# Attention with a threshold and a gated feed-forward: softmax tiles turned before they are normalised, the inverted sums sent through DRAM

## The chip, the cores and the metric

The kernel runs on one core of one Trainium2 chip. The metric is the time of one execution on the device in microseconds (us), the median of several runs. The engines are PE (TensorE; PEld is its weight load), DVE (VectorE), ACT (ScalarE), POOL (GpSimd) and SP (SyncE, which issues nearly all DMAs here).

## The reference

Eight batches, eight heads, 576 tokens, 64 elements a head; then a feed-forward from 512 to 1024 and back to 512 with a gate made by a convolution over three tokens.

```python
scores = scale * np.matmul(q, k.transpose(0, 1, 3, 2))
thresh = np.max(scores, axis=-1, keepdims=True) - tau
scores = np.where(scores >= thresh, scores, -1000000000.0)
scores = scores - np.max(scores, axis=-1, keepdims=True)
attn = np.exp(scores)
attn = attn / (np.sum(attn, axis=-1, keepdims=True) + 1e-09)
return np.matmul(attn, v).astype(np.float32)
...
h = np.maximum(x @ w_in, 0.0)
conv_out += conv_w[k][None, None, :] * hp[:, k:k + S, :]     # three taps over the tokens
gate = 1.0 / (1.0 + np.exp(-conv_out))
return (h * gate @ w_out).astype(np.float32)
```

A row in which no score reaches the threshold gets the same weight for every token.

## The kernel before, in words

**Tiles.** The 576 tokens of a batch are four tiles of 128 rows and one of 64. A batch is two chunks: the tiles 0 and 1 (256 rows), and the tiles 2, 3 and 4 (320 rows). The heads go in pairs, four pairs a batch; with a chunk a pair makes one of 64 entries `i` of the list `pairs`, and each of its tiles is a unit `u` (160 units). In a unit:

- `ps_s`: PE makes the scores of each of two heads (128 x 576, in PSUM; two buffers). In the first batch ("plain") q and k are used as float32, with the batches after that q and k are split in a high and a low part (`xq`, `q1`, `q2`, `ks`), whose pieces SP loads and moves.
- `few`: DVE takes each row's maximum (`top`, L599) and the threshold (`limit`, L605, on DVE, POOL or ACT). ACT makes the exponentials `em` (`exp`, L608), DVE multiplies with the comparison to the threshold and adds up the row (`mask`, L611).
- `guard` (L628), the reciprocal (L635) and `even` (L632) make a factor and, for empty rows, an addend; `norm` (L644, on POOL for 285 of 288 heads) applies both to `em`, in place.
- `transposes` (L703): PE turns `em` in blocks of 128 into `ps_t` (two buffers in PSUM), ACT copies them to `eT` (L698). In 28 units (`crossed`) it goes another way: ACT and POOL split `em` into its low and high 16 bits (`parts`, L326 and L328), SP stores them in DRAM (`rows`) and turns them by a DMA transpose into `eT`.

When all tiles of a pair are turned, `attend` multiplies `eT` with `v` into `pa` (L758, L767). `pa` takes its PSUM buffers from the same two as `ps_t`, and after the first two chunks two pairs go together (pairs 26 and 27, say), so both are in use then. ACT rounds the product into the high part of `x` (L774), DVE subtracts to get the low part (L777), and the buffer is free. With the four pairs of a chunk in `x`, `mm1` (`ph`, L795), the taps and gates (`hp`, `t`, L810 to L822), `gh`/`gl` and `mm2` (`po`, L853) make the feed-forward of that chunk, while the attention of the next runs.

**What sets the order.** `Plan` records every operation with its engine, its cost in ns, what it reads and writes, and a rank; `run` then simulates the engines with these costs and writes the instructions of each engine in the order that comes out. On the chip each engine and SP's queue go through their own list in that order. A buffer taken from a pool in turn (`em`, `few`, `ps_t`, ...) must be free first; operations with `other` may go to another engine when their own has more than a set amount waiting.

Of the kernel before, what the change touches and what calls it, by code (L numbers as in the profile page):

```python
# [10 lines left out]
F32 = mybir.dt.float32  # L11
# [9 lines left out]
HUGE = 3.0e38  # L21
AHEAD = {'s': 6.25, 's4': 7.75, 't': 3.5, 'a': 3.5, 'prep': 4.25, 'w': 2.5, 'load': 7.75}
# [5 lines left out]
NORM = (('pool',), ('pool',))  # L28

NEAR = 8  # L30
# [21 lines left out]
FAR = 3  # L52
XKS = 3
EMS = 5
# [200 lines left out]
def tile_tau_attention_gated_ffn(  # L255
# [307 lines left out]
    def unit(u, k, q1, q2, o, n):  # L563
# [7 lines left out]
        few = plan.buf(sm, "few", 4, [P, 8], F32, f"few_{u}")  # L571
        a = AHEAD["s" if 2 * n > P else "s4"]
        tiny = [("pool", 200)]
        for h, js in enumerate(heads):
            ps = plan.buf(ps_s, "ps_s", 2, [P, 2, 512], F32, f"ps_s_{u}_{h}")
            nm, th, total = (slice(at + h, at + h + 1) for at in (0, 2, 4))
# [33 lines left out]
            def mask(ps=ps, th=th, view=view, total=total):  # L610
                nc.vector.scalar_tensor_tensor(  # L611
                    view(), ps[:rows, :, :CH], few[:rows, th], view(), op0=ALU.is_ge, op1=ALU.mult,
                    accum_out=few[:rows, total]
# [9 lines left out]
            op("dve", 738, mask, w=[(em, h), (few, ("sum", h))], r=[(ps, 0), (few, ("th", h))], ahead=a)  # L623
        ss = [(few, ("sum", h)) for h in range(m)]
        sums, inverse, shift = slice(4, 4 + m), slice(6, 6 + m), slice(2, 2 + m)

        def guard(e):
            engines[e].tensor_scalar(few[:rows, inverse], few[:rows, sums], 1e-9, 1.0, op0=ALU.add, op1=ALU.mult)  # L628


        def even(e):
            engines[e].tensor_scalar(few[:rows, shift], few[:rows, sums], 0.0, 1.0 / S, op0=ALU.is_equal, op1=ALU.mult)  # L632

        op("dve", 112, guard, w=[(few, "inverse")], r=ss, ahead=a, port=True, other=tiny)
        op("dve", 82, lambda: nc.vector.reciprocal(few[:rows, inverse], few[:rows, inverse]), w=[(few, "inverse")], ahead=a)  # L635
        op("dve", 124, even, w=[(few, "shift")], r=ss, ahead=a, port=True, other=tiny)
        for h in range(m):
            def norm(e, h=h):
                sl = em[:rows, h * S:(h + 1) * S]
                by, to = few[:rows, 6 + h:7 + h], few[:rows, 2 + h:3 + h]  # L640
                if e == "act":
                    nc.scalar.activation(sl, sl, AF.Identity, scale=by, bias=to)
                else:
                    engines[e].tensor_scalar(sl, sl, by, to, op0=ALU.mult, op1=ALU.add)  # L644

            choice = {"pool": 807, "dve": 400, "act": 625}
            turns = NORM[u >= NEAR]
            home = turns[(u * 2 + h) % len(turns)]
            op(
# [368 lines left out]
```

## Time and profile before

| | |
|---|---|
| Median of three runs | 923.61 us (923.4 to 923.7) |
| Profiled execution | 925.83 us; its span, from the first to the last instruction, 924.0 us |
| PE, PEld | 883.6 us (96%), 709.9 us (77%) |
| DVE, ACT, POOL | 775.4 us (84%), 684.6 us (74%), 636.5 us (69%) |
| Granted TensorE clock | mean 0.989 |
| DMA | 122.28 MB in 120,927 packets, mean 132 GB/s |

The profile is one execution. A group's row gives line, engine, operation, output <- inputs with their shapes, the count, then busy us and mean ns of one, then the idle time of the engine before them with what ended it. A timeline row gives start, length and instruction, and in brackets the idle time before it with its releaser. A row of waits gives the sum, the number and the longest. DMA rows end with the median us from issue to landing.

### The profile page before, as it was taken

Reading aid. Unit: us, or ns where it says so; the run is one execution under the profiler, and the core shown is the slowest. Engines: PE = TensorE matmul, PEld = TensorE weight load, DVE = VectorE, ACT = ScalarE, POOL = GpSimd, SP = SyncE. Lnnn points to the kernel's source line nnn. Section 1 sums busy time; section 2 is a strip of 40 time slices with the busy share of each in tenths; the row PEclk is TensorE's granted clock in tenths of the full one; section 3 lists DMA queues with packets and bytes.
Section 4 is the critical chain, followed back from the end, with each engine's and each line's share of the span. In section 5 each row is a group of like instructions: output and inputs, shape, how many; then the busy total and the mean of one; then the engine's idle time right before and its main releaser. Section 6 shows DMA issues by size and latency. Waiting matters only on the chain.

```text
span 924.0 us, 18493 instructions
## 1 busy us (share of the span) xinstructions
PE 883.6 (96%) x6056; PEld 709.9 (77%) x6056; DVE 775.4 (84%) x1863; ACT 684.6 (74%) x1450; POOL 636.5 (69%) x1044
## 2 busy tenths in 40 slices
PE   5879899999999999999899999999999999999998
PEld 2445578768879788878778788887868878887897
DVE  5989999988998789987789779996979879998543
ACT  5868688778877787878668687877857778786643
POOL 3656867877777677876667778886866858785422
PEclk9989999999999999999899999999999999999999
DMA  5545137546563565526645275536647076543000
GB/s 207 168 152 158 44 113 210 120 132 181 141 172 76 153 178 158 148 73 175 166 123 126 86 183 138 158 92 181 169 114 180 29 194 169 131 120 100 14 23 35
DMA packets 120927, 122.28 MB, mean 132 GB/s; under 512 B 72320, under 2 KB 88960, under 8 KB 120832
## 3 DMA queue, kind: packets, MB, share of 16 engines
q1 hardware_dynamic: 119968, 119.20, 47.7%
q10 hardware_dynamic: 864, 1.90, 0.6%
q8 instruction: 49, 0.80, 0.4%
q14 instruction: 46, 0.38, 0.1%
HBM read 66.22 MB, written 25.95 MB: 100 GB/s over the span
## 4 chain that ended last, share of the span: by engine, by line
PE 63%; DVE 12%; ACT 10%; POOL 6%; DMA 5%; issue 4%; SPq 1%; ACTq 0%; DVEq 0%; POOLq 0%
PE po L853 17%; PE ph L795 13%; PE pa L767 10%; PE ps_s L591 9%; PE ps_t L703 9%; DVE em L611 4%; ACT em L608 3%; PE ps_s L584 3%; DVE few L599 3%; DMA xq<-in_qd_dram 2%; ACT eT L698 2%; POOL em L644 2%; PE pa L758 2%; DVE t L817 2%; DVE t L822 2%
## 5 line engine op out<-in xcount | busy, mean ns | idle before, releaser
L644 POOL TENSOR_SCALAR em<-em,few 128x576 f32<-128x576 f32 x285 | 258.5, 915 | 34.0 <-DVE few L635 22.4
L611 DVE SCALAR_TENSOR_TENSOR em<-ps_s,few,em 128x576 f32<-128x576 f32 x288 | 230.6, 812 | 38.2 <-ACT em L608 25.4
L608 ACT ACTIVATE em<-ps_s,few 128x576 f32<-128x576 f32 x288 | 210.4, 741 | 51.7 <-DVE few L599 43.1
L599 DVE TENSOR_REDUCE few<-ps_s 128x1 f32<-128x576 f32 x288 | 212.3, 749 | 35.5 <-PE ps_s L591 17.3
L795 PE MATMUL ph<-x,w1h 128*128 128x322 f32 (+1 forms) x1024 | 240.0, 306 | 0.9 <-ACT hp L810 0.6
L698 ACT ACTIVATE eT<-ps_t 128x512 f32<-128x512 f32 (+2 forms) x360 | 168.2, 487 | 31.2 <-PE ps_t L703 28.3
L795 PEld LDWEIGHTS ph<-x,w1h 128*128 128x128 f32 x1024 | 175.6, 191 | 6.3 <-issue 3.2
L703 PE MATMUL ps_t<-ident,em 128*128 128x128 f32 x1060 | 160.3, 280 | 9.6 <-POOL em L644 5.0
L591 PE MATMUL ps_s<-ks,q 128*128 128x288 f32 x896 | 158.9, 307 | 8.5 <-DVE em L611 5.9
L703 PEld LDWEIGHTS ps_t<-ident,em 128*128 128x128 f32 x1060 | 126.2, 143 | 34.4 <-POOL em L644 14.6
L795 PE MATMUL ph<-x,w1l 128*128 128x322 f32 (+1 forms) x512 | 151.9, 297 | 0.0
L591 PEld LDWEIGHTS ps_s<-ks,q 128*128 128x128 f32 x896 | 129.9, 190 | 26.7 <-issue 7.4
L333 POOL TENSOR_TENSOR gl<-t,gh 128x255 fp32r<-128x255 f32 (+9 forms) x192 | 122.7, 652 | 27.9 <-ACT gh L832 26.5
L767 PE MATMUL pa<-eT,v 128*64 128x320 f32 (+1 forms) x1024 | 132.1, 409 | 0.0
L853 PE MATMUL po<-w2h,gh 128*128 128x512 f32 x288 | 119.0, 413 | 0.4 <-ACT hp L810 0.4
L767 PEld LDWEIGHTS pa<-eT,v 128*64 128x64 f32 x1024 | 70.3, 137 | 59.4 <-issue 15.9
L853 PE MATMUL po<-w2h,gl 128*128 128x512 f32 x288 | 113.6, 395 | 0.2
L853 PE MATMUL po<-w2l,gh 128*128 128x512 f32 x288 | 113.5, 394 | 0.0
L817 DVE SCALAR_TENSOR_TENSOR t<-hp,cr 128x321 f32<-128x321 f32 (+1 forms) x128 | 85.1, 668 | 20.2 <-ACT hp L810 20.1
L795 PEld LDWEIGHTS ph<-x,w1l 128*128 128x128 f32 x512 | 97.7, 191 | 0.3
L817 DVE SCALAR_TENSOR_TENSOR t<-hp,cr,t 128x321 f32<-128x321 f32 (+1 forms) x128 | 91.9, 719 | 0.4
L824 ACT ACTIVATE t<-t,cm 128x321 f32<-128x321 f32 (+1 forms) x128 | 68.3, 534 | 28.3 <-DVE t L817 17.6
(81 smaller groups left out, 1147.9 us busy)
## 6 DMA issues: line engine op xcount, KB each, us to landing
v<-in_vc_dram SPq DMA_DIRECT2D x64, 288.0 KB, 3.9
rows<-parts SPq DMA_DIRECT2D x28, 576.0 KB, 3.2
k<-in_kp_dram SPq DMA_DIRECT2D x35, 320.0 KB, 3.5
out_dram<-ot SPq DMA_DIRECT2D x36, 256.0 KB, 2.1
xq<-in_qd_dram SPq DMA_DIRECT2D x28, 320.0 KB, 3.7
xk<-in_kt_dram SPq DMA_DIRECT2D x28, 288.0 KB, 3.3
ks<-xk SPq DMA_DIRECT2D x56, 144.0 KB, 3.6
xq<-in_qd_dram SPq DMA_DIRECT2D x28, 256.0 KB, 3.7
```

The costliest lines, as they stand in the source:

```text
L333: engines[e].tensor_tensor(dst, x, y, op=ALU.subtract)
L591: nc.tensor.matmul(ps[:, c, :CH], lhsT=q[:, h, o:o + n], rhs=k[:, h, c * CH:(c + 1) * CH], start=(i == 0), stop=(i == 1))
L599: nc.vector.tensor_reduce(few[:rows, nm], ps[:rows, :, :CH], op=ALU.max, axis=mybir.AxisListType.XY, negate=True)
L608: nc.scalar.activation(view(), ps[:rows, :, :CH], AF.Exp, bias=few[:rows, nm])
L611: nc.vector.scalar_tensor_tensor(view(), ps[:rows, :, :CH], few[:rows, th], view(), op0=ALU.is_ge, op1=ALU.mult, accum_out=few[:rows, total])
L644: engines[e].tensor_scalar(sl, sl, by, to, op0=ALU.mult, op1=ALU.add)
L698: "act", act(w, True), lambda dst=dst, src=src: nc.scalar.activation(dst(), src(pt), AF.Copy),
L703: nc.tensor.transpose(out=pt[:, at:at + P], in_=em[:, int(b * P):int(b * P) + P], identity=ident[:])
L767: nc.tensor.matmul(pa[j * D:(j + 1) * D, :w], lhsT=vt[:, blk, :], rhs=eT[:, :w // D, blk, :], start=False, stop=(r == 3))
L795: nc.tensor.matmul(ph[:, :an], lhsT=w1[w][:, cb, fs], rhs=xs[cb][:, h, :an], start=(cb == 0 and i == 0), stop=(cb == NCB - 1 and i == 2))
L817: nc.vector.scalar_tensor_tensor(t[:, :kn], hp[:, k:kn + k], cr[:, j, f:f + 1], y, op0=ALU.mult, op1=ALU.add)
L853: nc.tensor.matmul(po[:], lhsT=x[:, f, at:at + P], rhs=w[:, f, :], start=(f == 0 and i == 0), stop=(f == NFB - 1 and i == 2))
```

## The change

The row sums of a pair's units go into one small tile `tot` (a column for each head and tile) instead of each unit's `few`. `norm`, `even` and the per-unit guard and reciprocal go; PE turns `em` as it stands after `mask`. When a pair's units are recorded, `invert` adds a small number to all sums of the pair and inverts them (once a pair, 64 times); two DMAs (four with the chunk of 320 rows) store the columns as rows in DRAM, element by element, and two more load them back, each spread over the 64 partitions of one head (`inv`). In `attend`, DVE multiplies `pa` by `inv` into `xn` in SBUF, ACT rounds that into the high part of `x`, and POOL (or DVE) subtracts to get the low part. For empty rows ACT adds 2^-80 as it copies from `ps_t`; in the crossed units POOL takes the maximum of the high 16 bits with those of 2^-80, in place of a copy. There are four buffers of `em` instead of five.

```diff
+EVEN = 2.0 ** -80
+EVEN_TOP = 0x1780
-NORM = (('pool',), ('pool',))
-NEAR = 8
+INVS = 2
+PARTS = 2
-EMS = 5
+EMS = 4
@@ unit
                 nc.vector.scalar_tensor_tensor(
                     view(), ps[:rows, :, :CH], few[:rows, th], view(), op0=ALU.is_ge, op1=ALU.mult,
-                    accum_out=few[:rows, total]
+                    accum_out=tot[:rows, total]
                 )
...
-        op("dve", 112, guard, w=[(few, "inverse")], r=ss, ahead=a, port=True, other=tiny)
-        op("dve", 82, lambda: nc.vector.reciprocal(few[:rows, inverse], few[:rows, inverse]), w=[(few, "inverse")], ahead=a)
-        op("dve", 124, even, w=[(few, "shift")], r=ss, ahead=a, port=True, other=tiny)
-        for h in range(m):
-            def norm(e, h=h):
...
+    def invert(i, p, n, tot):
+        cols, a = 2 * (n // P) + (n % P > 0), AHEAD["a"]
+        spread = plan.buf(wk, "inv", INVS, [P, S - QW], F32, f"inv_{i}")
+        row = plan.buf(far, "row", INVS, [2, S - QW], F32, f"row_{i}")
+        ts = [(tot, j) for j in range(cols)]
         def guard(e):
+            engines[e].tensor_scalar(tot[:, :cols], tot[:, :cols], S * EVEN, 1.0, op0=ALU.add, op1=ALU.mult)
+
+        op("dve", 112, guard, w=ts, ahead=a, port=True, other=[("pool", 200)])
+        op("dve", 82, lambda: nc.vector.reciprocal(tot[:, :cols], tot[:, :cols]), w=ts, ahead=a)
+        for h in range(2):
+            def out(h=h):
+                nc.sync.dma_start(
+                    row[h, :n // P * P].rearrange("(t q) -> q t", q=P), tot[:, :n // P * 2].rearrange("q (t h) -> q t h", h=2)[:, :, h]
+                )
+
+            op("sp", 500, out, w=[(row, h)], r=ts, ahead=a, ring=n // P * P * 1.6)
+            if n % P:
+                op(
+                    "sp", 500, lambda h=h: nc.sync.dma_start(row[h, n // P * P:n].rearrange("(q e) -> q e", e=1), tot[h * D:(h + 1) * D, cols - 1:cols]),
+                    w=[(row, 2 + h)], r=ts, ahead=a, ring=D * 1.6
+                )
+        for h in range(2):
+            j = h ^ p % 2
+            put(
+                n, lambda h=h, j=j: nc.sync.dma_start(spread[j * D:(j + 1) * D, :n], row[h:h + 1, :n].broadcast_to([D, n])),
+                issue=500, rows=D, w=[(spread, j)], r=[(row, h)] + ([(row, 2 + h)] if n % P else []), ahead=a
             )
-        return em
+        return spread
@@ cross
-                copy(e, parts[:, j], src)
+                if j:
+                    engines[e].tensor_scalar(parts[:, j], src, EVEN_TOP, None, op0=ALU.max)
+                else:
+                    copy(e, parts[:, j], src)
@@ transposes
-                    "act", act(w, True), lambda dst=dst, src=src: nc.scalar.activation(dst(), src(pt), AF.Copy),
+                    "act", act(w, True), lambda dst=dst, src=src: nc.scalar.activation(dst(), src(pt), AF.Copy, bias=EVEN),
@@ attend
-            op("act", act(w, True), high, w=[(x, 0)], r=[(pa, 0)], ahead=a)
-            op("dve", dve(w), low, w=[(x, 1)], r=[(pa, 0), (x, 0)], ahead=a)
+            op("dve", dve(w), scale, w=[(xn, 0)], r=[(pa, 0), (inv, 0), (inv, 1)], ahead=a)
+            op("act", act(w), high, w=[(x, 0)], r=[(xn, 0)], ahead=a)
+            op("pool", pool(w), low, w=[(x, 1)], r=[(xn, 0), (x, 0)], ahead=a, other=[("dve", dve(w))], port=True)
@@ at the last tile of a pair
-                waiting.append((i, p, eT, vts[i], x, off))
+                waiting.append((i, p, eT, vts[i], x, off, invert(i, p, w, tot)))
```

The plan makes another order of it. Lines are those of each kernel by itself (L599, L605 and L611 of before are L601, L607 and L613 after; the scaling is L784, guard and reciprocal L636 and L639). Near the start, DVE's list before, in the units 2 and 3:

```order
L632 TENSOR_SCALAR few_2_195<-few_2_195 128x2
L599 TENSOR_REDUCE few_3_232<-ps_s_3_0_218 128x1
L635 RECIPROCAL few_2_195<-few_2_195 128x2
L599 TENSOR_REDUCE few_3_232<-ps_s_3_1_227 128x1
L389 SCALAR_TENSOR_TENSOR stage_0_f_151<-stage_0_105,stage_0_f_151 128x512
L611 SCALAR_TENSOR_TENSOR em_3_243,few_3_232<-ps_s_3_0_218,few_3_232,em_3_243 128x576
L611 SCALAR_TENSOR_TENSOR em_3_243,few_3_232<-ps_s_3_1_227,few_3_232,em_3_243 128x576
L777 TENSOR_TENSOR x_0_271<-pa_0_234,x_0_271 128x256
L632 TENSOR_SCALAR few_3_232<-few_3_232 128x2
L635 RECIPROCAL few_3_232<-few_3_232 128x2
```

and now (`stage` is a piece of the weights being unpacked):

```order
L601 TENSOR_REDUCE few_3_232<-ps_s_3_0_220 128x1
L639 RECIPROCAL tot_0_137<-tot_0_137 128x4
L384 TENSOR_SCALAR stage_1_f_181<-stage_1_f_181 128x512
L387 SCALAR_TENSOR_TENSOR stage_1_f_181<-stage_1_107,stage_1_f_181 128x512
L613 SCALAR_TENSOR_TENSOR em_3_240,tot_1_212<-ps_s_3_0_220,few_3_232,em_3_240 128x576
L601 TENSOR_REDUCE few_3_232<-ps_s_3_1_245 128x1
L390 SCALAR_TENSOR_TENSOR stage_1_f_181<-stage_1_107,stage_1_f_181 128x512
L601 TENSOR_REDUCE few_4_278<-ps_s_4_0_271 128x1
L613 SCALAR_TENSOR_TENSOR em_3_240,tot_1_212<-ps_s_3_1_245,few_3_232,em_3_240 128x576
L636 TENSOR_SCALAR tot_1_212<-tot_1_212 128x4
L639 RECIPROCAL tot_1_212<-tot_1_212 128x4
```

The reciprocal and the even of each unit are gone; a guard and a reciprocal come once for the two units of a pair, and the product of pair 0 is not taken from PSUM within these units any more.

In the fourth batch, where the pairs 26 and 27 are attended together, DVE's list before:

```order
L635 RECIPROCAL few_69_4783<-few_69_4783 128x2
L632 TENSOR_SCALAR few_69_4783<-few_69_4783 128x2
L817 SCALAR_TENSOR_TENSOR t_5_2_4823<-hp_5_2_4620,cr_509,t_5_2_4823 128x321
L611 SCALAR_TENSOR_TENSOR em_70_4852,few_70_4843<-ps_s_70_0_4826,few_70_4843,em_70_4852 128x576
L822 SCALAR_TENSOR_TENSOR t_5_2_4823<-t_5_2_4823,hp_5_2_4620 128x321
L632 TENSOR_SCALAR few_70_4843<-few_70_4843 128x1
L777 TENSOR_TENSOR x_26_4872<-pa_26_4835,x_26_4872 128x256
L635 RECIPROCAL few_70_4843<-few_70_4843 128x1
L817 SCALAR_TENSOR_TENSOR t_5_3_4902<-hp_5_3_4734,cr_509 128x321
L599 TENSOR_REDUCE few_71_4916<-ps_s_71_0_4888 128x1
L777 TENSOR_TENSOR x_27_4899<-pa_27_4838,x_27_4899 128x256
```

and now:

```order
L639 RECIPROCAL tot_27_4601<-tot_27_4601 128x4
L613 SCALAR_TENSOR_TENSOR em_69_4780,tot_28_4711<-ps_s_69_1_4759,few_69_4757,em_69_4780 128x576
L601 TENSOR_REDUCE few_70_4819<-ps_s_70_0_4804 128x1
L607 TENSOR_SCALAR few_70_4819<-few_70_4819,ntau_113 128x1
L601 TENSOR_REDUCE few_71_4842<-ps_s_71_0_4823 128x1
L831 SCALAR_TENSOR_TENSOR t_5_2_4848<-hp_5_2_4591,cr_439 128x321
L613 SCALAR_TENSOR_TENSOR em_70_4844,tot_28_4711<-ps_s_70_0_4804,few_70_4819,em_70_4844 128x576
L613 SCALAR_TENSOR_TENSOR em_71_4854,tot_29_4863<-ps_s_71_0_4823,few_71_4842,em_71_4854 128x576
L784 TENSOR_TENSOR xn_26_4874<-pa_26_4832,inv_26_4670 128x256
L831 SCALAR_TENSOR_TENSOR t_5_2_4848<-hp_5_2_4591,cr_439,t_5_2_4848 128x321
L831 SCALAR_TENSOR_TENSOR t_5_3_4887<-hp_5_3_4776,cr_439 128x321
L784 TENSOR_TENSOR xn_27_4905<-pa_27_4835,inv_27_4850 128x256
```

The reciprocal of pair 27 stands ten instructions ahead of the scaling that needs its inverse, and the masks of the next pairs' units 70 and 71 stand between.

At the same place, SP's list before:

```order
L541 DMA xq_30_4841<-in_qd_dram 128x2x320
L551 DMA k_30_4847<-in_kp_dram 128x640
L676 DMA rows_68_4861<-parts_68_4831 128x2304
L560 DMA v_28_4897<-in_vc_dram 128x576
L560 DMA v_29_4908<-in_vc_dram 128x576
L541 DMA xq_31_4911<-in_qd_dram 128x2x320
L681 DMA_TRANSPOSE eT_28_4923<-rows_68_4861 128x9x128 x2
```

and now (`row` is a store of inverted sums, `inv` their load):

```order
L642 DMA row_26_4563<-tot_26_4428 128x2x1
L655 DMA inv_26_4670<-row_26_4563 64x256 x2
L684 DMA rows_68_4778<-parts_68_4754 128x2304
L642 DMA row_27_4814<-tot_27_4601 128x2x1 x2
L542 DMA xq_30_4829<-in_qd_dram 128x2x320
L552 DMA k_30_4840<-in_kp_dram 128x640
L655 DMA inv_27_4850<-row_27_4814 64x256 x2
L542 DMA xq_31_4865<-in_qd_dram 128x2x320
L561 DMA v_28_4894<-in_vc_dram 128x576
L689 DMA_TRANSPOSE eT_28_4900<-rows_68_4778 128x9x128 x2
```

The stores and loads of the inverses stand among the loads of q and k, and the two of pair 27 behind `rows_68`.

More of the change, by code (lines that the diff above doesn't have):

```diff
@@ L672, in cross @@
                 home, choice[home], part, w=[(parts, j)], r=[(em, 0), (em, 1)], ahead=a, port=True,
-                other=[(e, ns) for e, ns in choice.items() if e != home]
+                other=[(e, ns) for e, ns in choice.items() if e != home and (e != "act" or not j)]
             )
@@ L927, in tile_tau_attention_gated_ffn @@
             at, n = TILES[t]
-            em = unit(now, *(whole[i] if n == P or i not in last else last[i]), at - o if n == P or i not in last else 0, n)
+            if t == tiles[0]:
+                tot = plan.buf(sm, "tot", 3, [P, 8], F32, f"tot_{i}")
+            em = unit(now, *(whole[i] if n == P or i not in last else last[i]), at - o if n == P or i not in last else 0, n, tot, 2 * ((at - o) // P))
             if t == tiles[0]:
```

42 lines of the change are left out of this document (15 added, 27 removed).

## The prediction

> **What bounds the kernel now.** I read the page's busy shares first, then the busy time by stretches, then PE's waits, then the groups of the lines that the change touches, and last SP's queue.
>
> ```profile
> PE 883.6 (96%) x6056; PEld 709.9 (77%) x6056; DVE 775.4 (84%) x1863; ACT 684.6 (74%) x1450; POOL 636.5 (69%) x1044
> ```
>
> PE works 883.6 of 924.0 us, and the change leaves its matmuls as they are (3878 rows in its order before and after). So nothing can be won beyond PE's 40.4 us of idle time and what its clock loses. The stretches tell where that is; after the length, the columns are the busy time of PE, PEld, DVE, ACT and POOL, then granted clock, DMA share and GB/s.
>
> ```profile
> 0.00:100.00 100.00, 80.75 (x456) 45.46 (x457) 83.50 (x201) 72.29 (x143) 55.32 (x89) 0.97 0.51 163
> 100.00:200.00 100.00, 91.58 (x629) 72.92 (x628) 95.68 (x233) 78.60 (x167) 76.47 (x121) 0.98 0.44 119
> 200.00:850.00 650.00, 640.83 (x4547) 530.49 (x4545) 562.37 (x1362) 499.11 (x1059) 483.81 (x791) 0.99 0.53 141
> ```
>
> PE's idle time is 19.25 us in the first 100, 8.42 in the second, 9.17 in the next 650, and 3.5, what is left of the 40.4, at the end. In the first two stretches DVE is the fuller engine (83.50 against 80.75; 95.68 against 91.58): there it sets the pace, and relief of DVE counts. From 200 on PE is busy 98.6%, and relief of any other engine counts only at a stall. Half of that idle time lies at two of them:
>
> ```profile
> 445.00:450.00 5.00, 3.88 (x34) 3.67 (x32) 3.37 (x7) 1.77 (x5) 0.88 (x3) 1.00 1.09 261
> 450.00:455.00 5.00, 3.66 (x15) 3.31 (x16) 4.62 (x13) 3.93 (x11) 4.29 (x7) 0.61 0.65 173
> 455.00:460.00 5.00, 5.00 (x32) 5.00 (x32) 3.02 (x6) 2.49 (x6) 3.49 (x5) 0.71 0.41 125
> 670.00:675.00 5.00, 3.75 (x23) 2.78 (x21) 2.30 (x5) 1.89 (x7) 2.62 (x4) 1.00 0.52 153
> 675.00:680.00 5.00, 4.12 (x15) 3.46 (x16) 3.99 (x12) 4.82 (x13) 2.88 (x7) 0.66 0.15 54
> 443.87 0.59 SPq L541 DMA_DIRECT2D xq<-in_qd_dram  x1
> 448.83 0.31 ACT L553 ACTIVATE q<-xq 128x128 f32<-128x128 f32 x1 [2.72 <-DMA xq<-in_qd_dram]
> 450.75 1.04 PE L591 MATMUL ps_s<-ks,q 128*128 128x288 f32 x4 [1.87 <-DVE em L611]
> ```
>
> A load of q was issued late, ACT stood 2.72 us in its order, DVE and then PE ran out of work, and the clock fell. The two stalls cost 4.6 us of idle time (1.12 + 1.34 + 1.25 + 0.88) and 5.1 us of clock (5 x (0.39 + 0.29 + 0.34)): 9.7 together.
>
> **The change part by part.** What goes:
>
> ```profile
> L644 POOL TENSOR_SCALAR em<-em,few 128x576 f32<-128x576 f32 x285 | 258.5, 915 | 34.0 <-DVE few L635 22.4 <-DVE few L605 10.1 <-DVE few L632 0.4
> L635 DVE RECIPROCAL few<-few 128x2 f32<-128x2 f32 (+1 forms) x160 | 25.4, 159 | 2.6 <-POOL few L628 1.6
> L628 DVE TENSOR_SCALAR few<-few 128x2 f32<-128x2 f32 (+1 forms) x72 | 22.6, 314 | 1.0
> L632 DVE TENSOR_SCALAR few<-few 128x2 f32<-128x2 f32 (+1 forms) x85 | 15.3, 180 | 0.0
> L628 POOL TENSOR_SCALAR few<-few 128x2 f32<-128x2 f32 (+1 forms) x88 | 23.8, 270 | 80.4 <-DVE em L611 77.5 <-DVE few L635 0.2
> L632 POOL TENSOR_SCALAR few<-few 128x2 f32<-128x2 f32 (+1 forms) x75 | 17.6, 235 | 34.8 <-DVE em L611 26.7 <-DVE stage_c_f L383 2.1 <-DVE few L635 2.0
> L605 DVE TENSOR_SCALAR few<-few,ntau 128x1 f32<-128x1 f32 x166 | 32.5, 207 | 0.8
> ```
>
> And the rows nearest to what comes:
>
> ```profile
> L777 DVE TENSOR_TENSOR x<-pa,x x64: 404/450/493, 25.3 to 875.1; 128x256 fp32r<-128x256 f32 x32, 128x320 fp32r<-128x320 f32 x32
> L333 POOL TENSOR_TENSOR gl<-t,gh 128x255 fp32r<-128x255 f32 x40 | 31.3, 781 | 11.9 <-ACT gh L832 11.6
> L333 POOL TENSOR_TENSOR gl<-t,gh 128x320 fp32r<-128x320 f32 x8 | 6.9, 868 | 0.3 <-ACT gh L832 0.3
> L328 POOL COPY parts<-em 128x1152 uint16<-128x1152 uint16 x27 | 32.8, 1216 | 0.6
> ```
>
> DVE loses 160 reciprocals, 72 guards and 85 evens (25.4 + 22.6 + 15.3 = 63.3 us). 41 limits (166 to 125 in the order) move to POOL: 41 x 0.207 = 8.5. It gains 64 reciprocals (x 0.159 = 10.2) and 15 guards (x 0.314 = 4.7). The scaling by the inverse stands in place of the subtraction of L777, with the same PSUM and SBUF inputs: 64 x 0.45 for 64 x 0.45. Net -56.9. POOL loses 258.5 + 23.8 + 17.6 and gains 64 subtractions (32 x 0.781 + 32 x 0.868 = 52.8), 49 guards (13.2) and 48 limits (about 17): net -217, to some 420. The maximum in place of the copy of parts is bounded by the copy (1.216) and two normalising instructions of 576 (1.83), 0 to +17 us in all; taken as the copy, which has the same tile. On ACT the reading of xn in place of pa and the added bias cost a few hundredths each, 2 us in all, hidden (ACT 74%). EMS 5 to 4 is at nothing: a tile of em no longer waits for guard, reciprocal and POOL.
>
> DVE's taps read two operands in SBUF, and their times scatter:
>
> ```profile
> L817 DVE SCALAR_TENSOR_TENSOR t<-hp,cr x128: 455/546/1641, 95.1 to 905.7; 128x255 f32<-128x255 f32 x64, 128x321 f32<-128x321 f32 x64
> L817 DVE SCALAR_TENSOR_TENSOR t<-hp,cr,t x128: 464/555/1630, 96.2 to 906.2; 128x255 f32<-128x255 f32 x64, 128x321 f32<-128x321 f32 x64
> ```
>
> The median is 0.09 us over the least, the longest 1.19 over; the two widths explain some, and what of the rest would go with POOL's work no row says. The sum takes none of it. The Trainium skill, page "SBUF — State Buffer", section "SBUF: two separate sides", calls the ports that VectorE shares with GpSimd an exclusive lock, held for a whole instruction. The scatter agrees; by that rule a third of the excess would go with a third of POOL's time: of the 32 or so taps in the second hundred us (2 x 128 over 810 us), at 0.09 us each, 1 us, and the sum below would come to 912.6.
>
> What comes on SP: 320 issues and a DRAM round trip per pair.
>
> ```profile
> out_dram<-ot SPq DMA_DIRECT2D x36, 256.0 KB, 2.1
> ks<-ks SPq DMA_DIRECT2D x28, 144.0 KB, 2.5
> L861 SPq DMA_DIRECT2D out_dram<-ot x36: 332/344/615, 144.5 to 921.2; - x36
> L510 SPq DMA_DIRECT2D ks<-ks x28: 461/518/866, 91.8 to 770.5; - x28
> SPq L676 <- ACT parts L326: 95.6, 19, 12.4
> q1 hardware_dynamic: 119968, 119.20, 47.7%
> ```
>
> Issues cost 320 x 0.34 to 0.52 = 110 to 166 us of SP's queue, which runs beside the rest. The bytes add 8% (128 x 64 rows of 1.0 or 1.25 KB: 9.4 MB on 119.2); the 36,864 writes of 4 bytes cost between nothing and a mean packet's time each (47.7% of 16 x 924 us over 119,968 is 59 ns), so the DMA share ends between 52 and 66%. From reciprocal to scaling the way is: two issues (0.9), landing 2.1 to 2.6, two more issues (1.0), landing 2.5 to 3.5: 6.5 to 8 us, estimated from these rows. In the order shown above for pair 27, DVE has ten instructions between its reciprocal and its scaling, some 6.9 us of work by the rows (three masks of 0.89, two reductions of 0.75, a limit, two taps, a scaling): the inverse comes about when it is asked for. For most pairs that distance is 9 to 28 us; for 14 of 64 it is under 9. There the scaling would wait, and behind it, in DVE's order, reductions and masks, and on PE the transposes, since both ps_t buffers hold the joint products.
>
> The terms, by stretches. DVE's small instructions at the start:
>
> ```profile
> L632 DVE TENSOR_SCALAR few<-few 128x2 f32<-128x2 f32 (+1 forms) x13 | 3.2, 247 | 0.0
> L635 DVE RECIPROCAL few<-few 128x2 f32<-128x2 f32 (+1 forms) x15 | 2.4, 157 | 0.0
> L628 DVE TENSOR_SCALAR few<-few 128x2 f32<-128x2 f32 (+1 forms) x4 | 1.7, 432 | 0.0
> ...
> L628 DVE TENSOR_SCALAR few<-few 128x2 f32<-128x2 f32 (+1 forms) x10 | 3.8, 383 | 0.1
> L635 DVE RECIPROCAL few<-few 128x2 f32<-128x2 f32 (+1 forms) x20 | 3.2, 160 | 0.0
> L632 DVE TENSOR_SCALAR few<-few 128x2 f32<-128x2 f32 (+1 forms) x16 | 2.5, 154 | 0.0
> ```
>
> - First 100 us: DVE sheds 7.3 and gets about 1.3 back (five pairs), and the way from mask to transposition loses a link of POOL (0.915). Ends: 0, if loads set the pace, and -8. Taken: -5, since DVE was the fuller engine.
> - 100 to 200: DVE sheds 9.5, gets 1.7 back. Ends: 0 and -8.4 (PE's whole idle time there). Taken: -5.
> - 200 to 850: ends 0 and -9.7, both stalls with their clock. POOL's queue, which frees the buffers of q, is a third shorter, SP's is longer; taken -2, the nearer end by far, since the load itself stays.
> - Waits for the inverse: -2 at best (the row below: PE waited once for L777 to free a product's buffer, which one instruction frees now, not two, where the inverse is there); +14 at worst (14 pairs, 1 us each). Taken +2, as DVE has 13% of slack there.
>
> ```profile
> PE ps_t L703 <- DVE x L777: 2.0, 1, 2.0
> ```
>
> Sum -10: a span of 914. The profiled run took 925.83 us, its span 924.0; the median of the runs is 923.61, 2.2 below it. I set the difference against the median: 913.6 us.
>
> **The rivals.**
> - Slower: the inverses hang behind other work on SP. The row of pair 27 stands behind rows_68, which waits for parts, and SP has waited for parts 95.6 us in 19 waits, up to 12.4. For it: SP takes its DMAs in order, and DVE and both ps_t buffers hang on the last of them. Against: in most pairs 9 us and more are in hand. It decides where the 14 tight pairs cost PE 0.9 us each, the 12 us won in the three stretches; with 1.5 us each, an inverse that lands some 10 us after its reciprocal, +21 - 12 gives 932.6.
> - No change: the start is paced by loads and the weights' preparation (DMA share 0.51 there), the middle by PE at 98.6%, and small waits eat the rest: 921.8 to 925.5.
> - More: both ends of the start and both stalls with their clock come true: -8 - 8.4 - 9.7 - 2 = -28, 895.6. For it: 1.6 us of normalising stood before each pair of heads on POOL. Against: the first 6 us are a load, and the late q waits for SP too.
>
> The granted clock was 0.66 from 50 to 60 and 0.84 from 110 to 120:
>
> ```profile
> 50.00:60.00 10.00, 8.25 (x33) 4.54 (x33) 7.45 (x18) 5.61 (x11) 5.02 (x8) 0.66 0.40 110
> 110.00:120.00 10.00, 9.74 (x59) 6.80 (x59) 9.07 (x25) 7.94 (x20) 4.75 (x13) 0.84 0.00 0
> ```
>
> The sum leaves these 5.0 us where they are. The Trainium skill, page "TensorE: Matmul & The Clock Gate", Part 1, says that PE drops to half rate after an idle window of about 3.4 us and comes back after a busy one; the stretches after both stalls (0.61, 0.66) agree. By that rule a fuller PE at the start would win them too, 908.6, and a new stall of DVE would cost its clock again.
>
> **How the numbers follow.** The forecast 0.54 (906 to 920 by itself), no change 0.14, slower 0.20, more 0.12. A measurement of this kernel tells about 0.2% from no change (1.85 us). Faster 0.68, same 0.12, slower 0.20. The range reaches from 901, most of the way to the larger gain, to 931, most of the way to the slower case's price.
>
> **What would show it.** PE's idle time in the first 200 us falls from 27.7 to about 18, with its busy time unchanged; POOL near 420 us, DVE near 715; 320 more issues on SP, landing in 2 to 3.5 us; waits of the scaling on the DMA of the inverse below 1 us but for a few; no clock below 0.9 after 200 us but once. It is wrong if DVE waits for the inverse by more than some 10 us in all, if the scaling's wait is what PE's transposes wait for, or if loads of q come later than now and stalls like the one at 449 come more often.

## The result, and the profile after

The changed kernel takes 1272.7 us (median of four runs, 1266.9 to 1278.1) against 923.65 for the kernel before beside it: ratio 1.378, 95% interval 1.372 to 1.384. The prediction was 913.6, range 901 to 931: wrong, with the change 349 us slower instead of 10 faster. One run of a later kernel (`before_light`), 1434.9 us at a mean granted clock of 0.561, was in a slow state and stays out of the medians. The page of the profile after: PE's busy time, the DMA queue with packets, MB and share of the span, and the chain that ended last, by engine and by line.

```profile
PE 977.8 (77%) x6056; PEld 775.8 (61%) x6056; DVE 731.4 (58%) x1583; ACT 684.6 (54%) x1440; POOL 471.2 (37%) x758
...
q1 hardware_dynamic: 170144, 128.80, 60.5%
...
DMA 39%; PE 30%; SPq 8%; ACT 8%; DVE 7%; issue 4%; POOL 2%; ACTq 0%; DVEq 0%; POOLq 0%
DMA row<-tot 13%; PE po L867 9%; DMA xq<-in_qd_dram 7%; PE ph L809 6%; DMA ks<-xk 5%; DMA xk<-in_kt_dram 5%; PE ps_s L593 5%; PE ps_t L711 4%; SPq L689 4%; PE pa L775 3%; DVE em L613 3%; DMA q<-in_qd_dram 2%; DMA inv<-row 2%; ACT em L610 2%; DVE few L601 1%
```

Of DVE's forecast relief of 57 us, 44 came (775.4 to 731.4), and they bought nothing: PE, busy 77% of the span, isn't the bound any more. DMAs are 39% of the chain, and first among them is the store of the inverted sums, 64 or 256 floats at a time, with 13%. Of the 347.6 us by which the span grew (924.0 to 1271.6), 253.4 are more idle time of PE (40.4 to 293.8), and 94.2 are longer busy time for the same 6056 matmuls, at a mean granted clock of 0.870 in place of 0.989. The stretches show both everywhere, not at the start alone (the third number from the end is the clock):

```profile
0.00:100.00 100.00, 63.30 (x297) 33.17 (x298) 56.53 (x133) 49.17 (x96) 19.63 (x51) 0.87 0.62 138
100.00:200.00 100.00, 65.64 (x403) 47.56 (x401) 59.04 (x124) 55.30 (x112) 35.98 (x53) 0.82 0.47 85
200.00:850.00 650.00, 508.13 (x3219) 411.58 (x3220) 382.04 (x825) 355.75 (x743) 257.21 (x395) 0.87 0.65 108
```

The waits of the whole run (sum, times, longest) tell what stood where:

```profile
SPq L655 <- DMA row<-tot: 342.7, 76, 10.4
...
DVE xn L784 <- DMA inv<-row: 127.8, 22, 16.8
...
ACT q L543 <- DMA xq<-in_qd_dram: 104.0, 19, 14.1
...
PE ps_t L711 <- DVE xn L784: 93.8, 21, 18.6
PE ps_s L593 <- DMA ks<-xk: 46.0, 7, 9.2
```

SP stands before the loads of `inv` until the stores have landed; DVE stands in its order before the scaling; PE's transposes wait for the PSUM buffer that the scaling frees. But ACT also waits 104 us for loads of q, and PE 46 us for pieces of k, which take no part in the sums. Before, the first of these two waits was almost nothing:

```profile
ACT q L542 <- DMA xq<-in_qd_dram: 1.8, 1, 1.8
```

SP's timeline at one pair of 320 rows, whose two heads have two stores each:

```profile
426.78 0.54 SPq L642 DMA_DIRECT2D row<-tot  x1
427.37 0.47 SPq L649 DMA_DIRECT2D row<-tot  x1
427.89 0.58 SPq L642 DMA_DIRECT2D row<-tot  x1
428.51 0.48 SPq L649 DMA_DIRECT2D row<-tot  x1
435.89 0.46 SPq L655 DMA_DIRECT2D inv<-row  x1
436.46 0.52 SPq L684 DMA_DIRECT2D rows<-parts  x1
...
437.56 0.84 SPq L655 DMA_DIRECT2D inv<-row  x1
```

The load issued at 435.89 is that of the first head, and it waits for that head's two stores, issued at 426.78 and 427.37: 9.1 and 8.5 us. The trace records the end of each of a store's 16 parts, and the last of these two stores came at 435.67 and 435.83. Over the stores of 256 floats whose 16 ends can be told apart (95 of 128), the median from issue to landing, worked out in the same way, is 10.1 us. The prediction had 2.1 to 2.6 for this landing. One more row differs from what was priced, POOL's maximum (least, median and longest ns):

```profile
L673 POOL TENSOR_SCALAR parts<-em x28: 3118/3122/3298, 170.7 to 1178.0; 128x1152 uint16<-128x1152 uint16 x28
```

### The profile page after: what moved, and what is told of

It reads as the page before. It is cut to its first block, busy times and chain, and to the rows that moved or that the text cites. A ratio compares the mean times of both kernels' runs of the same rounds, so it can differ in the third digit from the quotient of the medians.

```text
span 1271.6 us, 18297 instructions
## 1 busy us (share of the span) xinstructions
PE 977.8 (77%) x6056; PEld 775.8 (61%) x6056; DVE 731.4 (58%) x1583; ACT 684.6 (54%) x1440; POOL 471.2 (37%) x758
## 3 DMA queue, kind: packets, MB, share of 16 engines
q1 hardware_dynamic: 170144, 128.80, 60.5%
## 4 chain that ended last, share of the span: by engine, by line
DMA 39%; PE 30%; SPq 8%; ACT 8%; DVE 7%; issue 4%; POOL 2%; ACTq 0%; DVEq 0%; POOLq 0%
DMA row<-tot 13%; PE po L867 9%; DMA xq<-in_qd_dram 7%; PE ph L809 6%; DMA ks<-xk 5%; DMA xk<-in_kt_dram 5%; PE ps_s L593 5%; PE ps_t L711 4%; SPq L689 4%; PE pa L775 3%; DVE em L613 3%; DMA q<-in_qd_dram 2%; DMA inv<-row 2%; ACT em L610 2%; DVE few L601 1%
## 5 line engine op out<-in xcount | busy, mean ns | idle before, releaser
L601 DVE TENSOR_REDUCE few<-ps_s 128x1 f32<-128x576 f32 x288 | 212.2, 750 | 138.9 <-PE ps_s L593 102.9
L613 DVE SCALAR_TENSOR_TENSOR em<-ps_s,few,em 128x576 f32<-128x576 f32 x288 | 228.0, 812 | 104.3 <-ACT em L610 85.5
L711 PE MATMUL ps_t<-ident,em 128*128 128x128 f32 x1060 | 182.1, 308 | 137.4 <-DVE xn L784 93.8
L809 PE MATMUL ph<-x,w1h 128*128 128x322 f32 (+1 forms) x1024 | 248.4, 315 | 8.0 <-ACT hp L824 8.0
L711 PEld LDWEIGHTS ps_t<-ident,em 128*128 128x128 f32 x1060 | 142.1, 158 | 171.2 <-DVE xn L784 99.7
L593 PE MATMUL ps_s<-ks,q 128*128 128x288 f32 x896 | 176.8, 335 | 71.6 <-DMA ks<-xk 46.0
L593 PEld LDWEIGHTS ps_s<-ks,q 128*128 128x128 f32 x896 | 146.8, 216 | 90.0 <-DMA ks<-xk 47.6
L809 PEld LDWEIGHTS ph<-x,w1h 128*128 128x128 f32 x1024 | 183.8, 200 | 12.3 <-ACT hp L824 8.7
L607 POOL TENSOR_SCALAR few<-few,ntau 128x1 f32<-128x1 f32 x152 | 55.5, 367 | 258.4 <-DVE few L601 235.4
L784 DVE TENSOR_TENSOR xn<-pa,inv 128x256 f32<-128x256 f32 (+1 forms) x64 | 29.0, 454 | 173.7 <-DMA inv<-row 127.8
L867 PE MATMUL po<-w2h,gl 128*128 128x512 f32 x288 | 123.5, 429 | 5.8 <-POOL hp L821 3.0
L334 POOL TENSOR_TENSOR q<-xq,q 128x512 fp32r<-128x512 f32 x56 | 74.6, 1333 | 101.5 <-ACT q L543 100.2
```

Of the source, the lines that this page charges most:

```text
L334: engines[e].tensor_tensor(dst, x, y, op=ALU.subtract)
L593: nc.tensor.matmul(ps[:, c, :CH], lhsT=q[:, h, o:o + n], rhs=k[:, h, c * CH:(c + 1) * CH], start=(i == 0), stop=(i == 1))
L601: nc.vector.tensor_reduce(few[:rows, nm], ps[:rows, :, :CH], op=ALU.max, axis=mybir.AxisListType.XY, negate=True)
L607: engines[e].tensor_scalar(few[:rows, th], few[:rows, nm], -1.0, ntau[:rows], op0=ALU.mult, op1=ALU.add)
L613: nc.vector.scalar_tensor_tensor(view(), ps[:rows, :, :CH], few[:rows, th], view(), op0=ALU.is_ge, op1=ALU.mult, accum_out=tot[:rows, total])
L711: nc.tensor.transpose(out=pt[:, at:at + P], in_=em[:, int(b * P):int(b * P) + P], identity=ident[:])
```

## The experiments

**Is it SP's wait, or the stores themselves?** The first kernel keeps the stores and the order of every queue, but loads `inv` from a row of q:

```diff
-nc.sync.dma_start(spread[j * D:(j + 1) * D, :n], row[h:h + 1, :n].broadcast_to([D, n]))
+nc.sync.dma_start(spread[j * D:(j + 1) * D, :n], qd[0, 0, h:h + 1, 0, :n].broadcast_to([D, n]))
```

> The stores of the inverted sums stay as they are (36,864 writes of 4 bytes), but the loads of inv read a row of q instead of what was stored, so SP's queue no longer stands before them until a store has landed; the products are scaled by wrong numbers. The order of all five queues is that of the changed kernel. Theory H, the 4-byte writes hold the DMA engines and make every other transfer late: SP's 342.7 us of waiting for row go, but loads of q and k stay late and the time stays far above before, 1100 to 1250 us. Theory W, the stores are harmless to others and only SP's wait for their landing blocks the queue: 915 to 945 us. Theory L, the loads of inv or the mere number of DMAs cost: no better than 1200 us.

Measured: 1194.4 us (1192.6 to 1196.6), ratio 1.293 (1.289 to 1.298). So SP's wait is worth some 78 of the 349 us, and the larger part is there without it. Its waits:

```profile
DVE xn L784 <- DMA inv<-in_qd_dram: 86.4, 13, 14.6
...
ACT q L543 <- DMA xq<-in_qd_dram: 65.3, 18, 10.2
...
SPq L655 <- DMA row<-tot: 27.9, 7, 4.7
```

SP's 342.7 us before these loads fell to 27.9 that the profile still puts down to the stores. Yet DVE still waits 86.4 us for the loads of `inv`, which need no store now, up to 14.6 at a time, and ACT 65.3 us for those of q. Theory W (the stores are harmless) is out.

The second leaves the stores out as well:

```diff
-                nc.sync.dma_start(
-                    row[h, :n // P * P].rearrange("(t q) -> q t", q=P), tot[:, :n // P * 2].rearrange("q (t h) -> q t h", h=2)[:, :, h]
-                )
+                pass
...                                       # the store of the last 64 rows goes too; loads of inv from q
```

> The stores are left out altogether, and the loads of inv read a row of q; the products are scaled by wrong numbers. All else keeps the order of the changed kernel, less 192 issues on SP. This is what the rest of the change is worth. H and W: 905 to 935 us, near the forecast of 913.6 and not above the kernel before by more than 1%. L, the loads or the plan's new order cost by themselves: above 1000 us.

Measured: 938.6 us (937.8 to 941.2), ratio 1.017 (1.013 to 1.020). Theory L (the loads of `inv`, their bytes, the number of DMAs) is out: all 128 loads are here. The 256 us between these two kernels, which keep one order, are those of the stores with their 192 issues. And 938.6 is a little above what H allowed, 25 us above the forecast: something else in the change costs too (below).

**What about the stores?** 36,864 writes of 4 bytes, 16 to each 64 bytes of DRAM. The same stores with the elements apart (loads of `inv` from q again, the order of every queue the same):

```diff
-row = plan.buf(far, "row", INVS, [2, S - QW], F32, f"row_{i}")
+row = plan.buf(far, "row", INVS, [2, S - QW, P], F32, f"row_{i}")       # 512 bytes apart; then 16, 8, 4 and 2 in place of P
-row[h, :n // P * P].rearrange("(t q) -> q t", q=P)
+row[h, :n // P * P, 0].rearrange("(t q) -> q t", q=P)
...                                       # the store of the last 64 rows likewise
```

> As in the kernel whose loads read a row of q, but each 4-byte element is stored 512 bytes from the next, so no two writes of a store fall in one line. H, if writes to the same line of DRAM wait for each other: near the time without stores, 910 to 950 us. H, if each small write costs by itself: within 3% of the kernel with the same stores side by side. W: the same as that kernel, 915 to 945.

> As the kernel with the elements 512 bytes apart (947.5 us, against 1194.4 side by side), now 64 bytes apart. If writes wait for each other only within 64 bytes or less: 940 to 955 us. If within 512 bytes: eight elements still share one, and the time lies well above, 1050 to 1200.

> As the kernels with the elements 512 and 64 bytes apart (947.5 and 951.5 us, against 1194.4 side by side), now 32 bytes apart, two in 64 bytes. If writes wait for each other within 64 bytes: a part of the 243 us comes back, 960 to 1100. If only within 32 bytes or less: 945 to 955.

> As the other kernels with spaced elements, now 16 bytes apart, four in 64 bytes (one: 951.5 us, two: 959.2, sixteen: 1194.4). If the writes to one 64-byte line follow each other, the cost grows with each further one, 243/15 = 16 us a write: 3 x 16 + 951 = 1000, between 980 and 1020 us. If it jumps only with a full line: 955 to 970.

> The same with 8 bytes between the elements, eight in 64 bytes. If each further write to a line costs the same: 7 x 16 + 951 = 1063, between 1040 and 1100 us. If only full lines cost: 955 to 990. If elements that touch are what is slow: like the one with four.

| bytes from element to element | elements in 64 bytes | us | ratio to before (95%) |
|---|---|---|---|
| 512 | 1 | 947.5 | 1.026 (1.019 to 1.033) |
| 64 | 1 | 951.5 | 1.032 (1.030 to 1.035) |
| 32 | 2 | 959.2 | 1.039 (1.032 to 1.047) |
| 16 | 4 | 965.5 | 1.048 (1.045 to 1.051) |
| 8 | 8 | 1009.7 | 1.096 (1.092 to 1.099) |
| 4 | 16 | 1194.4 | 1.293 (1.289 to 1.298) |

The number of packets, their size, their issues and the order are the same in all six; only where the elements lie differs (two runs each, four of the last). So 243 to 247 us come from elements that lie closer than 64 bytes. The small packets with their 192 issues cost some 9 to 13 us (947.5 and 951.5 against 938.6; at 512 bytes the interval still overlaps that of the kernel without stores).

Where the price begins is less sharp. At 16 bytes it is clear of the kernel at 64 bytes. At 32 it isn't: 959.2 falls between the two forecasts, and its interval overlaps the other's, so whether 64 bytes or 32 are the unit is not settled. Nor does the time grow by a constant 16 us for each further element, as I had expected (965.5 for 1000, 1009.7 for 1063, outside all three forecasts); slack could hide the first delays, which isn't shown. The landing grows with each step. From the DMA views (size of the DMA, median us from issue to landing), elements 512, 32, 16 and 8 bytes apart:

```profile
xq<-in_qd_dram SPq DMA_DIRECT2D x28, 320.0 KB, 3.8
...
inv<-in_qd_dram SPq DMA_DIRECT2D x64, 80.0 KB, 3.2
...
row<-tot SPq DMA_DIRECT2D x128, 1.0 KB, 2.0
...
eT<-rows SPq DMA_TRANSPOSE x56, 4.1
```
```profile
row<-tot SPq DMA_DIRECT2D x128, 1.0 KB, 2.2
```
```profile
row<-tot SPq DMA_DIRECT2D x128, 1.0 KB, 3.3
```
```profile
xq<-in_qd_dram SPq DMA_DIRECT2D x28, 320.0 KB, 5.6
...
inv<-in_qd_dram SPq DMA_DIRECT2D x64, 80.0 KB, 5.9
...
row<-tot SPq DMA_DIRECT2D x128, 1.0 KB, 4.8
...
eT<-rows SPq DMA_TRANSPOSE x56, 6.6
```

From 2.0 to 4.8 us over seven further elements in 64 bytes is 0.40 us each on average, in uneven steps (0.2, then 0.55, then 0.38 us each). Fifteen further ones would make 8.0 us at that rate, an estimate; with the elements side by side (`unread`) the median is 9.2 us, over the 93 of 128 stores of 256 floats whose ends can be told apart in the trace. Writes close together behave as if they followed one another; that they do is not shown.

The last four rows against the first show that the delay isn't the stores' own: loads of q of 320 KB take 5.6 us in place of 3.8, turns of `eT` 6.6 in place of 4.1. The packets of the queue tell the same, with elements 512 bytes apart and side by side (`unread`):

```profile
q1 hardware_dynamic: 170144, 128.80, 51.2%
```
```profile
q1 hardware_dynamic: 170144, 128.80, 66.0%
```

Times the spans (949.5 and 1194.8 us) these shares are 486 and 789 us of each DMA engine, for the same packets. The additional time is not in the 4-byte packets: by the traces' records of single packets they take 9 and 10 ns on average. The queue's packets of 512 bytes and more take 104 and 186 ns on average, and what grows is a few of them: 36 last over 1 us in the first kernel, 1726 in the second, and of these 89% lie within 10 us after the issue of a store, in stretches that make up 59% of the span. So packets of other transfers stand still, most of them while a store lands.

The Trainium skill, page "DMA: Bandwidth & Descriptors", section "Specifications", says that transfers under 512 bytes are made by reading, changing and writing back. By that rule alone the kernels with elements 512 and 4 bytes apart would pay alike; the measurement says that the price comes where several such writes lie closer than 64 bytes. That the reading and writing back is the reason is not shown.

**A store without small writes.** The computation in full: DVE turns the inverted sums in blocks of 32 x 32, and each store moves two or four rows of 128 bytes, 1152 in all; the plan is given a second tile and one store for each tile and head (a part of the edit):

```diff
+op("dve", 130, lambda: nc.vector.transpose(turned[i % 2][:], tot[:]), w=[(turned[i % 2], 0)], r=ts, ahead=a)
...
+nc.sync.dma_start(row[h, t * P:(t + 1) * P].rearrange("(b q) -> b q", q=32), turned[i % 2][2 * t + h:P:32, :])
```

> The computation of the changed kernel in full, but DVE first turns the inverted sums in blocks of 32 (64 more small instructions), so that a store writes two or four pieces of 128 bytes instead of 128 or 256 of 4: 1152 packets in place of 36,864, with 4 or 6 issues a pair on SP in place of 2 or 4. SP still waits for the landing of each store. H: 915 to 960 us, since what is left is the wait of one plain round trip. W: the wait stays, 1150 to 1280 us. L: 1200 us or more, as there are more DMAs.

Measured: 948.2 us (947.2 to 949.3), ratio 1.027 (1.023 to 1.031): 324 us of the 349 are back, with more issues and the whole round trip. DVE's waits for the inverses shrink from 127.8 us to 6.6:

```profile
DVE xn L792 <- DMA inv<-row: 6.6, 4, 3.3
```

**The other 25 us.** The kernel without stores, and with POOL copying `parts` in place of taking the maximum (empty rows not shared; the same order):

```diff
-engines[e].tensor_scalar(parts[:, j], src, EVEN_TOP, None, op0=ALU.max)
+copy(e, parts[:, j], src)
```

> The kernel without stores (loads of inv from a row of q), and in the crossed units a plain copy by POOL in place of the maximum, so empty rows are not shared; every queue has the same order. In the kernel without stores the maximum took 3.18 us where the copy of before took 1.22, 28 times, 55 us of POOL, and the time was 938.6, 14.4 above before. Theory M, the slow maximum makes POOL's later limits and SP's stores of rows late: 918 to 929 us. Theory O, the plan's other order, with the four buffers of em, is what costs: 934 to 940, as without this edit.

Measured: 915.9 us (912.8 to 919.8), ratio 0.993 (0.991 to 0.996), just below theory M's range; theory O is out. With the order as it is, the maximum costs 2.3% of the time, 22.7 us, though POOL is busy half of the time only. The stretch from 200 on, without stores and then also without the maximum:

```profile
200.00:850.00 650.00, 626.93 (x4445) 520.96 (x4445) 528.22 (x1136) 488.97 (x1037) 358.55 (x550) 0.99 0.55 149
```
```profile
200.00:850.00 650.00, 640.45 (x4586) 535.31 (x4583) 532.79 (x1166) 499.55 (x1062) 319.06 (x557) 1.00 0.56 152
```

PE gets back 13.5 of its idle us there. The plan prices the instruction at 1.26 us, and it takes 3.16 to 3.18; what needs POOL next waits. Three edits of the turned kernel tried to make it cheaper or to tell the plan: bfloat16 in place of integers; the plan's price; the maximum on DVE, first as a choice and then always (the last two also set the plan's prices).

```diff
+engines[e].tensor_scalar(parts[:, j].bitcast(mybir.dt.bfloat16), src.bitcast(mybir.dt.bfloat16), EVEN, None, op0=ALU.max)   # turned_bf
+choice = {"act": act(2 * S), "pool": 3160.0 if j else pool1(2 * S), "dve": dve(2 * S)}                                  # turned_true
+home = ("act", "dve")[j]                                                                                                 # turned_dve, turned_force
```

> The kernel with the sums turned by DVE (948.2 us), in which POOL takes the maximum of the same 16 bits read as bfloat16 instead of as integers; the same order, the computation in full. If the integer type is what makes it 3.18 us against 1.22 for the copy: 925 to 935 us. If a maximum costs that in any type: 945 to 951.

> The kernel with the sums turned by DVE (948.2 us), in which the plan is told that POOL takes 3.16 us for the maximum, not 1.26; the computation in full. The order changes with it. If the plan's wrong price for it is part of what is lost: 930 to 942 us. If not: 945 to 952.

> The kernel with the sums turned, in which DVE takes the maximum instead of POOL, and the plan knows that POOL would take 3.16 us; the computation in full, with a new order. If POOL's long instruction is what costs: 915 to 930 us. If the wait for the round trip of the inverses costs as much: 930 to 945.

> The kernel with the sums turned, in which DVE takes the maximum in all 28 crossed units (8 of 28 in the kernel before this one, at 1.11 us each, and 929.6 us); the computation in full, with a new order. If POOL's instruction of 3.18 us is all that keeps it behind: 912 to 922 us, as the kernel without stores and maximum (915.9). If the round trip of the inverses costs some 10 us of its own: 923 to 932.

Measured: bfloat16 948.5 us (1.027, 1.022 to 1.031), no help, as the group's row says (mean 3179 ns); the true price 930.5 (1.009, 1.007 to 1.012); on DVE as a choice 929.6 (1.008, 1.005 to 1.010); on DVE always 928.5 (1.010, 1.007 to 1.013).

```profile
L681 POOL TENSOR_SCALAR parts<-em 128x1152 bf16<-128x1152 bf16 x28 | 89.0, 3179 | 19.5 <-DVE em L613 19.4
```
```profile
L681 DVE TENSOR_SCALAR parts<-em 128x1152 uint16<-128x1152 uint16 x8 | 8.8, 1106 | 0.0
```
```profile
L681 DVE TENSOR_SCALAR parts<-em 128x1152 uint16<-128x1152 uint16 x28 | 23.8, 850 | 0.1
```

DVE takes 1.11 us for it in the 8 units of 28 that the plan gave it, and 0.85 on average where it has all 28. The last three kernels give back 18 to 20 us. The one with the true price does so with all 28 maxima still on POOL, at 3.19 us: most of the price was not the instruction itself but an order made with a wrong cost for it. The three stay 0.8 to 1.0% behind the kernel before. To see whether that rest is SP's wait for the stores' landing, the last of them with the loads of `inv` from a row of q:

> The kernel with the sums turned and the maximum on DVE (928.5 us), but the loads of inv read a row of q, so SP doesn't wait for the stores of the turned sums; the products are scaled by wrong numbers; the order is the same. If SP's wait for their landing (about 2 us, 64 times) holds the loads behind it: 914 to 922 us. If the order and the additional instructions make the difference: 925 to 931.

Measured: 929.9 us (929.0 to 930.6), ratio 1.009 (1.007 to 1.011). It isn't: the time is the same, and DVE waits as long for the loads of `inv` as with the stores in front of them (7.1 us in 4 waits against 6.9 in 4). That leaves the order, the turning (64 times 0.21 us on DVE) and the additional issues. Which of them was not settled.

**What the rest of the change is worth.** The kernel before without its normalisation, the order of every queue the same (the sums divide nothing):

```diff
-engines[e].tensor_scalar(few[:rows, inverse], few[:rows, sums], 1e-9, 1.0, op0=ALU.add, op1=ALU.mult)
-engines[e].tensor_scalar(few[:rows, shift], few[:rows, sums], 0.0, 1.0 / S, op0=ALU.is_equal, op1=ALU.mult)
-nc.vector.reciprocal(few[:rows, inverse], few[:rows, inverse])
-engines[e].tensor_scalar(sl, sl, by, to, op0=ALU.mult, op1=ALU.add)
...                                       # norm's other form, on ACT, goes too
```

> The kernel before without its normalisation: norm, even, guard and reciprocal are left out, so the sums divide nothing; every queue keeps the order of before. It tells what the relief of DVE (63 us) and POOL (300 us) is worth by itself. If it is worth what the prediction's first three terms said (-5, -5, -2): 909 to 915 us. If the start is paced by loads and the middle by PE: 920 to 925.

Measured: 915.9 us (913.4 to 917.1, five runs), ratio 0.992 (0.989 to 0.995), that is 4 to 10 us. Its stretches:

```profile
0.00:100.00 100.00, 81.07 (x478) 46.73 (x479) 80.02 (x175) 73.24 (x146) 27.73 (x51) 1.00 0.52 168
100.00:200.00 100.00, 93.32 (x655) 73.39 (x655) 90.59 (x193) 80.63 (x169) 40.98 (x72) 1.00 0.46 129
200.00:850.00 650.00, 641.28 (x4557) 535.11 (x4554) 527.96 (x1130) 496.36 (x1061) 247.64 (x437) 0.99 0.52 140
...
50.00:60.00 10.00, 7.86 (x42) 4.09 (x44) 9.50 (x21) 6.96 (x14) 2.44 (x4) 1.00 0.38 122
110.00:120.00 10.00, 9.78 (x66) 6.49 (x66) 9.85 (x20) 8.42 (x21) 3.28 (x9) 1.00 0.35 113
```

PE's idle time fell by 0.3, 1.7 and 0.5 us, not by 5, 5 and 2. What PE waited for in the first hundred us, before and then here:

```profile
PE ps_s L584 <- DVE em L611: 6.9, 7, 1.8
PE ps_s L584 <- ACT q L500: 6.5, 1, 6.5
```
```profile
PE ps_s L584 <- DVE em L611: 7.4, 8, 1.7
PE ps_s L584 <- ACT q L500: 7.0, 1, 7.0
```

The first load, which ACT waits for, and the masks of DVE cost as much with a DVE that has less to do. Of the 9.9 us by which this profile's span is shorter (924.0 to 914.1), 7.4 are shorter busy time of PE (883.6 to 876.2); the clock of the two stretches that the sum left out was 0.66 and 0.84 before and is 1.00 here. One profile of each doesn't show that the relief brought the clock: the runs of the kernel before that were taken beside these differ too, from 927.6 us at a mean clock of 0.989 to 920.7 at 0.998, and at 0.996, the clock of this profile, it took 921.2.

Last, one number of the change alone, `EMS = 5` to `EMS = 4` in the kernel before:

> The kernel before, with four buffers of em instead of five, and the order that the plan makes of that; nothing else of the change. If the lost buffer is what the kernel without stores pays: 932 to 942 us. If not (M, or another part of the order): 921 to 929.

Measured: 915.6 us (914.4 to 917.0), ratio 0.993 (0.991 to 0.995), with the computation in full. It is faster than the kernel before and the changed one, and outside both forecasts. The edit changes the number of buffers and, with it, the plan's order; since a buffer less can only add waits, the order must be what helps, though no run takes the two apart:

```profile
100.00:200.00 100.00, 94.30 (x640) 74.32 (x638) 91.19 (x224) 81.34 (x171) 80.31 (x128) 0.97 0.45 122
200.00:850.00 650.00, 643.95 (x4603) 536.23 (x4600) 570.92 (x1387) 504.42 (x1084) 479.42 (x772) 1.00 0.53 142
```

PE's idle time from 200 to 850 is 6.0 us in place of 9.2, and in the second hundred 5.7 in place of 8.4.

## Why the prediction was wrong

- **The step that failed: the landing of the stores.** It was priced at 2.1 to 2.6 us from stores of 256 KB and moves of 144 KB, whose rows are long pieces, and the 36,864 packets at 0 to 59 ns each by the share of time that DMA engines are busy. The runs showed 9 to 10 us of landing in its place, with elements side by side, and other transfers standing still meanwhile; with the elements 512 bytes apart the landing is 2.0 us, as the prediction had it. The packets themselves were within their price (9 to 11 ns). The busy share came out at 60.5%, inside the forecast's 52 to 66, but by luck: that forecast was for a span of 924 us, at most 610 us of each DMA engine, and 60.5% of 1271.6 are 769. The nearest row by kind (a store) was not the nearest by what mattered (many writes into one place), and no row of before showed that; the upper end of the range should have said so.
- **"SP's queue runs beside the rest".** The issues did. The wait behind them didn't: 342.7 us of SP standing before the loads of `inv`, worth 78 us. And the delay reached loads that had no part in the change; unread against nostore, 256 us. No term of the sum had a place for it.
- **Waits for the inverse, +2 (-2 to +14).** Measured 127.8 us of DVE in 22 waits. With the sums turned it is 6.6 us in 4 waits, under the 10 that the prediction had named as a sign of being wrong, and force_unread gains nothing by taking the stores' part of it away. So the term fits the kernel whose stores are rows.
- **The slower rival** named the mechanism (the inverse late, DVE and both ps_t buffers hang on it, the clock falls), and all three signs that the prediction set against itself came. Its price, +21, counted only the 14 tight pairs and an inverse 10 us late; it had no other transfers in it.
- **First and second hundred us, -5 and -5; from 200, -2.** By itself the relief is worth 4 to 10 us, not far from the 12, but not by the way that the sum took, and so by luck: 0.3, 1.7 and 0.5 us of idle time. DVE was the fuller engine in both stretches, but PE waited in the first hundred for the first load and the masks as long as before. Being the busiest engine didn't make DVE the one that sets the pace. The clock, which the sum left alone and a sentence behind it put at 5 us by the Trainium skill, page "TensorE: Matmul & The Clock Gate", Part 1, was at 1.00 in the profile of before_light, but from 50 to 60 only at 0.83 in that of nomax, which sheds the same work. In the changed kernel PE's busy time grew by 94.2 us.
- **The maximum as a copy, 0 to +17 us of POOL.** It takes 3.16 us, not 1.22 to 1.83: +54 us of POOL, and 22.7 us of the time in the order that the plan made with 1.26. That POOL had room (some 420 of 914 us) didn't hide it: in the kernel without stores DVE's masks wait 4.2 us for limits on POOL, ACT 4.5 us and SP 37.3 us for the maximum itself; without the maximum these are 1.0, 0 and 2.0.
- **EMS 5 to 4 at nothing.** In the kernel before, it gives -0.7% by itself: a gain, not a cost. In the changed kernel no run takes it back.
- **Two slips that change nothing.** The list between reciprocal and scaling of pair 27 names two taps where the order shows three; its 6.9 us hold with three. The 1.6 us of normalising before a pair of heads are 2 x 0.915 = 1.83 by the row.

In one chain of kernels, from before to the changed one, the steps are -6 for the rest of the change with its order (nomax), +23 for the maximum, +9 for the packets with their issues, +247 for elements side by side and +78 for SP's wait: 351, measured 349. As differences along one chain they must add up, and another order of taking things away could divide them differently.

## What to carry to other kernels

A store that writes single floats side by side in DRAM is to be priced by how close the elements lie (at 16 bytes and less it cost clearly more here), not by its bytes or packets; turn the data on the chip first (one 0.21-us instruction here), so that each packet is a row of 128 bytes. Price a new instruction from a row with the same operation and type on the same engine, since a maximum isn't a copy, and give a planner that price: the order that it made with the right one won back 18 us with the slow instruction in place. Where a planner sets the order, run its parameters alone: one number gave as much (915.6 us) as the whole rest of the change with its order (915.9).

## What the runs showed of the hardware that I had not expected

- A store of 256 single floats landed in 2.0 and 1.9 us with the elements 512 and 64 bytes apart in DRAM, in 2.2, 3.3 and 4.8 at 32, 16 and 8 bytes, and in 9.2 side by side; other transfers landed later with it (`eT` 4.1 us at 512 bytes, 6.6 at 8).
- The 4-byte packets took 9 to 11 ns whether they lay apart or side by side. What grew was single packets of other transfers: 36 of over 1 us with the elements 512 bytes apart, 1726 side by side.
- The busy share of a DMA queue hides this when the span grows too: 51.2% and 66.0% are 486 and 789 us of each engine for the same packets.
- POOL takes 3.16 to 3.19 us for a maximum with a constant over 128 x 1152 values of 16 bits, integers or bfloat16 alike, where it copies them in 1.22; DVE takes 0.85 to 1.11.
